# Quad 4's scores in whole tiles, quad 3's denominators ahead of them, and one load of values on another queue

## The chip, the cores and the metric

The kernel runs on one core of a Trainium2 chip. The metric is the device time of one execution in microseconds, the median of several runs. Every time below is in microseconds from the start of the profiled span unless it says otherwise.

## What is computed

Attention with a forget gate over 8 batches, 8 heads, 576 positions and 64 columns a head, then a two-layer network with a GELU on the result, seen as 4608 rows of 512:

```python
scores = (q @ k.T) / sqrt(64) + cum[:, None] - cum[None, :]    # cum = cumsum(log(clip(f, 1e-4, 1)))
attn = softmax(where(causal, -1e9, scores))
x = (attn @ v).transpose(0, 2, 1, 3).reshape(4608, 512)
h = x @ w_in                                                   # 512 x 2048
out = gelu_tanh(h) @ w_out                                     # 2048 x 512
```

## The kernel before

**Tiling.** The attention goes in 16 quads of four heads of one batch; quad i belongs to batch i // 2 and holds heads 0 to 3 (i even) or 4 to 7 (i odd). The two layers go in nine chunks of 512 rows. Chunks and quads are interleaved: the second layer of a chunk (the word F or f) is cut into small units that are put between the steps of the quads.

**The steps of a quad i**, with their words in the tables and their engines:

- LK.i, LQ.i load keys and queries through the queue of POOL (GpSimd); TK.i, TQ.i transpose them on DVE (VectorE), L197. LV.b.h loads half the heads' values of batch b through the queue of SP, LX.b.h does the same load through POOL's queue; both are five transfers, L168.
- S.i.r makes round r of the scores (r = 0, 1, 2, of 512 columns each) on PE (TensorE), L261. The four heads of a quad lie in four groups of 32 rows, and a matmul of a head uses only its own 32 rows of the array (32*128 in the profile). The result stands in two tiles of two heads each; ACT (ScalarE) takes each tile's exponential into the buffer pt (L269). H.i.r.g does the same for one pair of heads g alone. Q.i.r.g does the whole round, with pair g in a tile of another pool.
- M.i.r masks what lies beyond the diagonal on POOL (L275), m.i.r does it on DVE (L301).
- vw.i or VW.i (DVE or POOL, L214) scales the values by the gates; CL.i or cl.i copies a part of the result (L219).
- D.i sums the denominators on PE (L326), then transposes, inverts and transposes back on DVE (L345 to L349).
- V.i.x and v.i.x make the value products on PE (L326), and DVE multiplies them with the inverted denominators into xT (L357).

**The layers.** I.c.p is a product of the first layer of chunk c, 8 matmuls of 512 columns (L371) and a GELU of 1024 columns on ACT (L378). The second layer of chunk 0 has 64 units (L646): a unit of F is one matmul over the whole array, a unit of f is four matmuls of 32 columns each. Every 16 units give a block of output, which DVE copies (L652) and SP stores (L653).

**Tiles of PSUM.** Three pools hold the eight banks. psS has two tiles of two banks each, which the scores, the first layer (L371) and the product v.i.x take in turn. psO has one tile of two banks, which D.i and V.i.x share. psM has two tiles of one bank, for the second layer. A tile is taken again when its reader is done.

**Order.** The order of all work is written out by hand: FRONT (L73) for the time until chunk 1's first layer, and TABLES for the rest. Each engine and each DMA queue carries out its instructions in the order of the words. A word with @ waits until the transfer, or the step, named behind it is done: LX.1.1@WO.2 starts when the piece WO.2 of w_out has landed, VW.3@m.3.1 after the mask m.3.1.

What the change touches: the order in FRONT, the words H, S, Q (scores, L242), I (mlp_in, L360, where `spare` puts the tile into psO), LX and LV (load_v, L164).

Of the kernel before, what the change touches and what calls it, by code (L numbers as in the profile page):

```python
# [16 lines left out]
def kernel(  # L17
# [12 lines left out]
    B, H, S, D = q.shape  # L30
# [44 lines left out]
        H.1.0.1 H.1.0.0 vw.1.0 D.0.0 M.1.0.1 M.1.0.0 LP.3 WI.4 WI.5 B.2.384 H.1.1.1 V.0.0.0 H.0.1.1 V.0.1.0 H.0.1.0 D.1.0 V.1.0.0 M.0.1 WI.6 WI.7  # L75
        H.1.1.0 V.1.1.0 M.1.1 Q.0.3.0 h.0.0.0 h.0.0.0 M.0.3 LQ.2 LK.2 Q.1.3.1 h.0.0.1 h.0.0.1 vw.0.1 S.1.2 M.1.3@vw.0.1 VW.1.1 WO.0 D.0.1 j.0.1 j.0.1
        j.0.1 j.0.1 E.0.0 j.0.1 V.0.1.1 V.0.0.1 D.1.1 J.0.2 WO.1 V.1.1.1 V.1.0.1 J.0.3 w.1 J.1.0 WO.2@WI.7 WO.3 J.1.1 TQ.2 LK.3 LQ.3 J.1.2 J.1.3
        LX.1.0@WO.0 LQ.4 TK.2 X F.0.7 LK.4 TK.3 S.2.0 M.2.0 LK.5 F.0.9 S.2.2 M.2.2 LX.1.1@WO.2 F.0.10 S.2.1 TQ.3 F.0.9 LV.2.0@LK.5 m.2.1 vw.2 S.3.0
        f.0.1 CL.2 LQ.5 M.3.0 D.2 TK.4 f.0.6 S.3.1 F.0.6 m.3.1 VW.3@m.3.1 V.2.0 TQ.4 S.3.2 TK.5 LK.6 M.3.2 f.0.7 V.2.1 S.4.1 LQ.6 F.0.6 TQ.5 CL.3
        H.4.2.1 D.3 H.4.0.1 LQ.7 VW.4 H.4.0.0 V.3.1 v.3.0 f.0.3 H.4.2.0 CL.4 I.1.0 m.4.1 U.0 LV.2.1@LQ.5 I.1.4 TQ.6 m.4.2.3 I.1.1 I.1.5 U.1  # L80
        LV.3.0@LQ.7 LV.3.1 m.4.2.2 TK.6 G.0 M.4.0 LK.7 LQ.8 LK.8 I.1.2 I.1.3 U.3 K.1.0 K.1.1 K.1.2 I.1.6 I.1.7 G.1.1.2 U.2 X F.1.16 S.5.0 f.1.26 S.5.1
        D.4 M.5.0 f.1.16 S.5.2 V.4.0 m.5.2.3 f.1.10 VW.5 V.4.1 K.1.3 CL.5 m.5.2.2 S.6.0 f.1.10 M.5.1 D.5 f.1.7 S.6.1 V.5.1 f.1.12 V.5.0 T.2 S.6.2 vw.6
    """

    HOMES = {1: 0, 3: 1, 0: 2}
# [41 lines left out]
    def many(n, shape, dtype, name):  # L127
        return [singles.tile(shape, dtype, name=f"{name}{i}") for i in range(n)]
# [10 lines left out]
    vw = many(2, [128, NT + 1, 4, D], BF16, "vw")  # L139
# [15 lines left out]
    spare = singles.tile([1, 1], FP32, name="spare")  # L155
# [204 lines left out]
    def mlp_in(c, prs, spare=0):  # L360

        if spare:
            tiles = [psO.tile([128, 1024], FP32, name="ps_h", tag="po").rearrange("p (a n) -> p a n", a=2) for _ in prs]
        else:
            tiles = [psS.tile([128, 2, 512], FP32, name="ps_h", tag="s") for _ in prs]
        for pr, ph in zip(prs, tiles):
            for dts in (range(N_DT - 1), range(N_DT - 1, N_DT)):
                for j in range(2):
                    ft = 2 * pr + j
                    for dt in dts:  # L370
                        nc.tensor.matmul(  # L371
                            ph[:, j, :],
                            w_in_sb[:, dt, 128 * ft:128 * ft + 128],
                            xT[:, dt, CH * c:CH * (c + 1)],
                            start=(dt == 0), stop=(dt == N_DT - 1),
                        )
        for pr, ph in zip(prs, tiles):
            nc.scalar.activation(gT[:, 2 * pr:2 * pr + 2, :], ph, AF.Gelu_apprx_tanh)  # L378
# [111 lines left out]
    def mlp_in_half(half, g, spare=0):  # L490

        if spare:
            ph = psO.tile([128, 1024], FP32, name="ps_h", tag="po").rearrange("p (a n) -> p a n", a=2)
        else:
            ph = psS.tile([128, 2, 512], FP32, name="ps_h", tag="s")
        n0 = QA * half
        for j in range(4):
            ft = 4 * g + j
            for dt in range(N_DT):
                nc.tensor.matmul(  # L500
                    ph[:, j // 2, QA * (j % 2):QA * (j % 2) + QA],
                    w_in_sb[:, dt, 128 * ft:128 * ft + 128],
                    xT[:, dt, n0:n0 + QA],
                    start=(dt == 0 and j % 2 == 0), stop=(dt == N_DT - 1),
                    skip_group_check=True,
                )
            if j < 3:
                yield
        if spare:
            yield  # L510
        nc.scalar.activation(gT[:, 4 * g:4 * g + 4, n0:n0 + QA],
                             ph.rearrange("p a (b n) -> p (a b) n", n=QA), AF.Gelu_apprx_tanh)
# [212 lines left out]
    def pull(it, n):  # L725
        for _ in range(n):
            if next(it, False) is False:
                return
# [14 lines left out]
    def load_values(b, half):  # L743
# [29 lines left out]
        "LP": lambda t: load_v(0, ts=(t,), eng=nc.gpsimd),  # L773
        "WI": load_w_in,
        "WO": load_w_out,
        "I": lambda c, pr: mlp_in(c, (pr,)),
        "J": lambda half, g: pull(mlp_in_half(half, g), 4),
        "j": lambda half, g: pull(parts_in.setdefault((half, g), mlp_in_half(half, g, 1)), 1),
        "Q": lambda i, r, *other: scores(i, r, other=other),
# [90 lines left out]
```

## Time and profile before

| what | value |
|---|---|
| median of 3 runs | 318.97 (318.74 to 319.11) |
| the profiled execution | 319.03 |
| its span, first to last instruction | 317.3 |
| PE busy | 310.3 (98%) |
| DVE busy | 249.0 (78%) |
| ACT busy | 206.6 (65%) |
| POOL busy | 116.8 (37%) |

By stretch, around the change (busy time of each engine, share of the DMA engines): from 40.0 to 48.0, PE 7.84, DVE 4.47, ACT 5.66, POOL 6.09, DMA 1.08; from 48.0 to 56.6, PE 8.40, DVE 8.46, ACT 5.82, POOL 5.42, DMA 0.92; from 56.6 to 63.2, PE 6.48, DVE 5.44, ACT 4.92, POOL 5.79, DMA 0.90.

How to read it: the busy times of the engines overlap. The chain of waits goes back from the last instruction to what released it, step by step, and so gives the work that set the end. The busy time of an engine off that chain costs nothing by itself. A row of the timeline or of the chain has its start, its length, the engine, the line, and what is written from what; "x16" counts matmuls, and a few per cent of matmul records are missing.

### The profile page before, as it was taken

How to read it: one execution, taken by the hardware profiler on the slowest of the kernel's cores; microseconds unless marked ns; L12 is line 12 of the kernel's file. 1: busy time of each engine (PE TensorE's matmuls, PEld its weight loads, DVE VectorE, ACT ScalarE, POOL GpSimd, SP SyncE). 2: the span in 40 equal slices, each digit the busy share in tenths (PEclk: the TensorE clock that was granted, in tenths of full speed). 3: DMA queues.
4: the chain of work that ended last, by engine and by line, in shares of the span. 5: the costliest groups of instructions: out<-in, count | busy, mean ns of one | idle time of the engine just before them, and what ended most of it. 6: DMA issues, size and time to landing. Idle time of an engine off the chain costs nothing.

```text
span 317.3 us, 12367 instructions
## 1 busy us (share of the span) xinstructions
PE 310.3 (98%) x5533; PEld 218.6 (69%) x5553; DVE 249.0 (78%) x398; ACT 206.6 (65%) x266; POOL 116.8 (37%) x165
## 2 busy tenths in 40 slices
PE   8999999999999999999999999999999999999995
PEld 4468744545776477766867777768767788788784
DVE  6776059877789899779987998689878878886872
ACT  4795777676766786759756865778567844723730
POOL 8996475820500219601770068104850240000000
PEclk9999999999999999999999999999999999999999
DMA  7999999898104820791149512971120102013013
GB/s 127 230 200 199 206 225 230 171 193 175 43 22 127 138 65 19 151 222 33 37 97 197 111 37 68 170 168 37 37 68 0 37 25 80 3 34 101 0 35 99
DMA packets 47573, 33.45 MB, mean 105 GB/s; under 512 B 29856, under 2 KB 42272, under 8 KB 47520
## 3 DMA queue, kind: packets, MB, share of 16 engines
q0 software_dynamic: 9712, 15.99, 29.0%
q1 hardware_dynamic: 37664, 16.60, 19.8%
q8 instruction: 43, 0.70, 0.9%
q14 instruction: 10, 0.08, 0.1%
q10 hardware_dynamic: 144, 0.07, 0.1%
HBM read 36.85 MB, written 9.44 MB: 146 GB/s over the span
## 4 chain that ended last, share of the span: by engine, by line
PE 93%; DMA 2%; DVE 1%; issue 1%; POOL 1%; ACT 0%; POOLq 0%; DVEq 0%
PE ps_w L574 31%; PE ps_h L371 16%; PE po L326 10%; PE ps_s L261 9%; PE ps_cd L431 8%; PE ps_ab L431 6%; PE pso L646 4%; PE ps_h L500 4%; DMA q_c<-in_q_dram 2%; PE ps_h L385 2%; PE po_m L312 1%; PE ps_q L523 1%; PE ps_o L326 0%; DVE qT L197 0%; POOL k_c L191 0%
## 5 line engine op out<-in xcount | busy, mean ns | idle before, releaser
L269 ACT ACTIVATE pt<-ps_s 128x1024 bf16<-128x1024 f32 (+2 forms) x98 | 92.4, 992 | 36.2 <-PE ps_s L261 31.8
L275 POOL TENSOR_SCALAR_AFFINE_SELECT pt<-pt 128x512 bf16<-128x512 bf16 (+2 forms) x69 | 40.5, 597 | 100.3 <-ACT pt L269 99.2
L371 PE MATMUL ps_h<-xT,w_in_sb 128*128 128x512 bf16 x228 | 54.5, 379 | 0.6
L574 PEld LDWEIGHTS <-gT 128*32 128x32 bf16 (+1 forms) x1247 | 50.5, 97 | 6.0 <-issue 1.7
L574 PE MATMUL ps_w<-w_out_sb,gT 128*32 128x256 bf16 (+1 forms) x1050 | 46.9, 273 | 0.0
L378 ACT ACTIVATE gT<-ps_h 128x1024 bf16<-128x1024 f32 x30 | 30.6, 1019 | 19.5 <-PE ps_h L371 19.3
L371 PEld LDWEIGHTS <-w_in_sb 128*128 128x128 bf16 x240 | 23.4, 98 | 24.3 <-issue 0.4
L574 PEld LDWEIGHTS <-gsum 128*32 128x32 bf16 (+1 forms) x1256 | 39.1, 97 | 1.5
L261 PE MATMUL ps_s<-qT,kT 32*128 32x448 bf16 (+5 forms) x880 | 35.0, 261 | 0.6 <-DVE qT L197 0.4
L214 POOL TENSOR_TENSOR vw<-v_nat,wT 128x1280 bf16<-128x1280 f32 (+1 forms) x13 | 29.8, 2290 | 4.1 <-DVE xT L357 3.0
L574 PE MATMUL ps_w<-usum,gsum 128*32 128x256 bf16 (+1 forms) x832 | 30.5, 273 | 0.0
L197 DVE STREAM_TRANSPOSE kT<-k_c 128x576 f32<-128x576 f32 x16 | 19.9, 1241 | 11.8 <-DMA k_c<-in_k_dram 11.8
L599 DVE TENSOR_TENSOR o_st<-ps_w,snap 128x512 f32<-128x512 f32 x31 | 21.2, 686 | 9.7 <-PE ps_w L574 8.1
L261 PEld LDWEIGHTS <-kT 32*128 32x128 bf16 x896 | 15.9, 92 | 17.2 <-issue 12.0
L431 PEld LDWEIGHTS <-w_in_sb 128*128 128x128 bf16 x240 | 23.5, 98 | 5.7
L440 ACT ACTIVATE gT<-snap 128x512 bf16<-128x512 f32 x45 | 26.2, 627 | 0.6
L357 DVE TENSOR_TENSOR xT<-po,rb 128x576 bf16<-128x576 f32 x26 | 19.5, 750 | 3.8 <-PE po L326 3.2
L326 PE MATMUL po<-pt,vw 128*32 128x64 bf16 (+4 forms) x624 | 22.4, 278 | 0.0
L326 PEld LDWEIGHTS <-vw 128*32 128x32 bf16 x672 | 14.0, 96 | 10.5 <-issue 4.1
L431 PEld LDWEIGHTS <-xT 128*128 128x128 bf16 x180 | 17.6, 98 | 4.4
L197 DVE STREAM_TRANSPOSE qT<-q_c 128x576 f32<-128x576 f32 x16 | 19.9, 1243 | 0.7 <-DMA q_c<-in_q_dram 0.7
L191 POOL DMA_DIRECT2D k_c<-in_k_dram x16 | 9.2, 577 | 25.0 <-DVE qT L197 21.0
(115 smaller groups left out, 485.9 us busy)
## 6 DMA issues: line engine op xcount, KB each, us to landing
out_dram<-o_st SPq DMA_DIRECT2D x35, 256.0 KB, 2.5
k_c<-in_k_dram POOLq DMA_DIRECT2D x16, 288.0 KB, 6.1
q_c<-in_q_dram POOLq DMA_DIRECT2D x16, 288.0 KB, 6.8
v_nat<-in_v_dram SPq DMA_DIRECT2D x16, 256.0 KB, 6.5
v_nat<-in_v_dram SPq DMA_DIRECT2D x20, 128.0 KB, 5.7
w_in_sb<-in_moe_w_in_dram POOLq DMA_DIRECT2D x8, 256.0 KB, 6.3
w_out_sb<-in_moe_w_out_dram POOLq DMA_DIRECT2D x4, 512.0 KB, 9.7
v_nat<-in_v_dram POOLq DMA_DIRECT2D x9, 128.0 KB, 7.3
```

Source lines behind the costliest of these rows:

```text
L197: nc.vector.transpose(out=dst.rearrange("p s c -> p (s c)").bitcast(FP32) .rearrange("p (t a) -> p a t", a=S // 32), in_=src.rearrange("p ...
L214: return eng.tensor_mul(vw[i % 2][:, t0:t1], vb[:, t0:t1, h0:h0 + 4, :], wT[:, i, t0:t1, :].unsqueeze(3).to_broadcast([128, t1 - t0, 4, D]))
L261: nc.tensor.matmul(tiles[h // 2][:, h % 2, c0:c0 + nq], key_columns(i, key, h, c), qq[32 * h:32 * h + 32, q0:q0 + nq, c], start=(c == 0 an ...
L269: nc.scalar.activation(p[:, 2 * g:2 * g + 2, off:off + n], t[:, :, 0:n], AF.Exp, scale=scale)
L275: return nc.gpsimd.affine_select(out=x, in_=x, compare_op=ALU.is_ge, fill=0.0, base=0, pattern=pattern, channel_multiplier=-1)
L326: nc.tensor.matmul(po[r0:r0 + w.shape[-1], 448 + q0:448 + q0 + nq], w, p[:, h, col:col + nq], start=(key in (0, "low")), stop=(key in ("lo ...
L371: nc.tensor.matmul(ph[:, j, :], w_in_sb[:, dt, 128 * ft:128 * ft + 128], xT[:, dt, CH * c:CH * (c + 1)], start=(dt == 0), stop=(dt == N_DT ...
L378: nc.scalar.activation(gT[:, 2 * pr:2 * pr + 2, :], ph, AF.Gelu_apprx_tanh)
L431: nc.tensor.matmul(ps[:, j], w[:, dt, 128 * j:128 * j + 128], x[:, dt], start=(first and j == 0 and dt == 0), stop=(dt == 1), skip_group_c ...
L440: nc.scalar.activation(gT[:, ft:ft + 2, HC * j:HC * (j + 1)], x, AF.Gelu_apprx_tanh)
L574: nc.tensor.matmul(ps[c0:c0 + width, n, cols[0]:cols[1]], x[:, j, 128 * n + c0:128 * n + c0 + width], w[:, j, cols[0]:cols[1]], start=(fir ...
L599: nc.vector.tensor_add(st, ps, kept[name])
```

## The change

In FRONT:

1. Around quad 4, the four half scores H.4.2.1, H.4.0.1, H.4.0.0 and H.4.2.0 become two whole ones, S.4.2 and Q.4.0.1. Q.4.0.1 has heads 2 and 3 in the tile of psO. D.3 comes ahead of S.4.2. The nine units of the second layer there (F.0.6 and f.0.3) are cut into F.0.3, F.0.2, f.0.2 and f.0.2.
2. TQ.5 and LQ.7 move behind the product v.3.0. M.3.2 moves ahead of LK.6.
3. I.1.1 becomes I.1.1.1: its tile is taken from psO instead of psS. For that, the word I gets the argument `spare`.
4. The units of the second layer ahead of S.2.2 and of S.2.1 change places: F.0.10 and F.0.9 instead of F.0.9 and F.0.10.
5. LX.1.1@WO.2, the load of the second half of batch 1's values, becomes LV.1.1@WO.3: through SP's queue instead of POOL's, and after another piece of w_out.

The number of units of the second layer is 64 before and after.

```diff
-LX.1.0@WO.0 LQ.4 TK.2 X F.0.7 LK.4 TK.3 S.2.0 M.2.0 LK.5 F.0.9 S.2.2 M.2.2 LX.1.1@WO.2 F.0.10 S.2.1 TQ.3 F.0.9 LV.2.0@LK.5 m.2.1 vw.2 S.3.0
-f.0.1 CL.2 LQ.5 M.3.0 D.2 TK.4 f.0.6 S.3.1 F.0.6 m.3.1 VW.3@m.3.1 V.2.0 TQ.4 S.3.2 TK.5 LK.6 M.3.2 f.0.7 V.2.1 S.4.1 LQ.6 F.0.6 TQ.5 CL.3
-H.4.2.1 D.3 H.4.0.1 LQ.7 VW.4 H.4.0.0 V.3.1 v.3.0 f.0.3 H.4.2.0 CL.4 I.1.0 m.4.1 U.0 LV.2.1@LQ.5 I.1.4 TQ.6 m.4.2.3 I.1.1 I.1.5 U.1
+LX.1.0@WO.0 LQ.4 TK.2 X F.0.7 LK.4 TK.3 S.2.0 M.2.0 LK.5 F.0.10 S.2.2 M.2.2 LV.1.1@WO.3 F.0.9 S.2.1 TQ.3 F.0.9 LV.2.0@LK.5 m.2.1 vw.2 S.3.0
+f.0.1 CL.2 LQ.5 M.3.0 D.2 TK.4 f.0.6 S.3.1 F.0.6 m.3.1 VW.3@m.3.1 V.2.0 TQ.4 S.3.2 TK.5 M.3.2 LK.6 f.0.7 V.2.1 S.4.1 LQ.6 F.0.3 CL.3 D.3 F.0.2
+S.4.2 VW.4 V.3.1 f.0.2 v.3.0 TQ.5 LQ.7 f.0.2 Q.4.0.1 CL.4 I.1.0 m.4.1 U.0 LV.2.1@LQ.5 I.1.4 TQ.6 m.4.2.3 I.1.1.1 I.1.5 U.1 LV.3.0@LQ.7 LV.3.1
...
-        "I": lambda c, pr: mlp_in(c, (pr,)),
+        "I": lambda c, pr, spare=0: mlp_in(c, (pr,), spare),
```

More of the change, by code (lines that the diff above doesn't have):

```diff
@@ L77 @@
         j.0.1 j.0.1 E.0.0 j.0.1 V.0.1.1 V.0.0.1 D.1.1 J.0.2 WO.1 V.1.1.1 V.1.0.1 J.0.3 w.1 J.1.0 WO.2@WI.7 WO.3 J.1.1 TQ.2 LK.3 LQ.3 J.1.2 J.1.3
-        LX.1.0@WO.0 LQ.4 TK.2 X F.0.7 LK.4 TK.3 S.2.0 M.2.0 LK.5 F.0.9 S.2.2 M.2.2 LX.1.1@WO.2 F.0.10 S.2.1 TQ.3 F.0.9 LV.2.0@LK.5 m.2.1 vw.2 S.3.0
-        f.0.1 CL.2 LQ.5 M.3.0 D.2 TK.4 f.0.6 S.3.1 F.0.6 m.3.1 VW.3@m.3.1 V.2.0 TQ.4 S.3.2 TK.5 LK.6 M.3.2 f.0.7 V.2.1 S.4.1 LQ.6 F.0.6 TQ.5 CL.3
-        H.4.2.1 D.3 H.4.0.1 LQ.7 VW.4 H.4.0.0 V.3.1 v.3.0 f.0.3 H.4.2.0 CL.4 I.1.0 m.4.1 U.0 LV.2.1@LQ.5 I.1.4 TQ.6 m.4.2.3 I.1.1 I.1.5 U.1
-        LV.3.0@LQ.7 LV.3.1 m.4.2.2 TK.6 G.0 M.4.0 LK.7 LQ.8 LK.8 I.1.2 I.1.3 U.3 K.1.0 K.1.1 K.1.2 I.1.6 I.1.7 G.1.1.2 U.2 X F.1.16 S.5.0 f.1.26 S.5.1
-        D.4 M.5.0 f.1.16 S.5.2 V.4.0 m.5.2.3 f.1.10 VW.5 V.4.1 K.1.3 CL.5 m.5.2.2 S.6.0 f.1.10 M.5.1 D.5 f.1.7 S.6.1 V.5.1 f.1.12 V.5.0 T.2 S.6.2 vw.6
+        LX.1.0@WO.0 LQ.4 TK.2 X F.0.7 LK.4 TK.3 S.2.0 M.2.0 LK.5 F.0.10 S.2.2 M.2.2 LV.1.1@WO.3 F.0.9 S.2.1 TQ.3 F.0.9 LV.2.0@LK.5 m.2.1 vw.2 S.3.0
+        f.0.1 CL.2 LQ.5 M.3.0 D.2 TK.4 f.0.6 S.3.1 F.0.6 m.3.1 VW.3@m.3.1 V.2.0 TQ.4 S.3.2 TK.5 M.3.2 LK.6 f.0.7 V.2.1 S.4.1 LQ.6 F.0.3 CL.3 D.3 F.0.2
+        S.4.2 VW.4 V.3.1 f.0.2 v.3.0 TQ.5 LQ.7 f.0.2 Q.4.0.1 CL.4 I.1.0 m.4.1 U.0 LV.2.1@LQ.5 I.1.4 TQ.6 m.4.2.3 I.1.1.1 I.1.5 U.1 LV.3.0@LQ.7 LV.3.1
+        m.4.2.2 TK.6 G.0 M.4.0 LK.7 LQ.8 LK.8 I.1.2 I.1.3 U.3 K.1.0 K.1.1 K.1.2 I.1.6 I.1.7 G.1.1.2 U.2 X F.1.16 S.5.0 f.1.26 S.5.1 D.4 M.5.0 f.1.16
+        S.5.2 V.4.0 m.5.2.3 f.1.10 VW.5 V.4.1 K.1.3 CL.5 m.5.2.2 S.6.0 f.1.10 M.5.1 D.5 f.1.7 S.6.1 V.5.1 f.1.12 V.5.0 T.2 S.6.2 vw.6
     """
```

## The prediction, made before the changed kernel was run

> **What bounds the kernel now.** I read the page first, then the chain that ended last, then each engine's timeline from 40 to 80 us, and the DMA view in short windows. The chain:
>
> ```profile
> PE 93%; DMA 2%; DVE 1%; issue 1%; POOL 1%; ACT 0%; POOLq 0%; DVEq 0%
> ```
>
> TensorE sets the end; the clock row is full throughout. So an edit counts by what it does to PE's sequence, or by a new wait in it. Around the change the chain is PE without a break:
>
> ```profile
> 55.99 0.57 PE ps_s L261 x16
> 56.56 0.16 issue
> 56.72 1.24 PE pso L646 x5
> 57.96 0.56 PE ps_s L261 x7
> 58.52 0.80 PE po L326 x24
> 59.32 1.08 PE ps_s L261 x18
> 60.40 0.80 PE po L326 x24
> 61.19 0.73 PE ps_o L326 x24
> 61.92 0.65 PE pso L646 x12
> 62.57 0.56 PE ps_s L261 x8
> 63.13 0.32 PE ps_h L371
> ```
>
> In words of the table these are S.4.1, F.0.6 (two rows), H.4.2.1, D.3, H.4.0.1 with H.4.0.0, V.3.1, v.3.0, f.0.3, H.4.2.0 and the start of I.1.0. (Some matmul records are missing, so counts fall short of 24 or 6.) A half score of two heads (0.56) costs as much as a whole one of four (0.57): the heads sit in different rows of the array and run side by side, so half a score leaves half the rows empty. At 17.4 us a whole score with its tiles in two pools (ps_s and ps_so) runs its heads interleaved likewise.
>
> **The reworked stretch.** Prices: F.0.10 took 2.26 us (42.47 to 44.73) and F.0.6 1.40 (56.56 to 57.96), so a unit of the second layer is 0.86/4 = 0.215 and entering it from narrow work costs 0.11. f units are 0.65/3 = 0.217. Products take 0.80 after a score or an F, 0.68 after an f (55.31 in the chain). A whole score takes 0.57, its round 0 with 24 matmuls 0.63 (47.42 and 78.85).
>
> - Before, end of S.4.1 to I.1.0: 63.13 - 56.56 = 6.57.
> - After: F.0.3 0.75, D.3 0.80, F.0.2 0.54, S.4.2 0.57, V.3.1 0.80, f.0.2 0.43, v.3.0 0.68, f.0.2 0.43, Q.4.0.1 0.63 = 5.63.
>
> That is 0.94 less: four half scores (2.20) become two whole ones (1.20), two products lose a little, and one more entry into F costs 0.11. The nine units of F and f are the same work.
>
> Now the waits. S.4.2 needs both score buffers, so both exponentials of S.4.1, which end at 58.53 (ACT runs them 0.97 each from 56.59); PE gets there at 56.56 + 2.09 = 58.65. Cover 0.1. V.3.1 needs the product tile that D.3's transpose on DVE reads: D.3 ends at 58.1, the transpose takes 0.78, PE arrives at 59.2. Cover 0.3; DVE is free then, since TQ.5 (1.23) now stands behind it and DVE idled 0.95 there before. v.3.0 needs S.4.2's first exponential: 60.25 against PE's 60.45. Q.4.0.1 needs the second one (61.2) and the product tile (V.3.1's multiplication, 60.9), PE arrives at 61.56. Each is covered, none by more than 0.7. Each cover that fails costs its shortfall.
>
> Then the first layer. ACT's four exponentials end at 64.0 or so, as before (64.19), then a table load of 1.28; so the first GELU starts near 65.3, hardly earlier than 65.51. PE is about 1 us earlier, so it needs room: I.1.1 in the product tile gives it a third buffer. Three products of 1.73 from 62.0 end at 67.2, the first GELU at 66.3. Cover 0.9.
>
> **The two words before it.** At S.2.2 PE waits:
>
> ```profile
> 41.59 0.25 PE ps_s L261 x2
> 41.83 0.00 issue
> 41.84 0.63 PE ps_s L261 x8
> ```
>
> From 41.59 to 42.47 is 0.88 where a whole score takes 0.57: 0.31 goes on ACT's exponential, which ends at 41.78. F.0.10 ahead of it in place of F.0.9 puts 0.215 of work into that wait, and the unit is missing after it: 0.21 gained, if S.2.1 finds its buffers free (its exponentials end at 44.46, PE would come at 44.5). Between nothing and 0.21 I take 0.21.
>
> **The load that changes queue.** LX.1.1, five loads of v on POOL (3.63 us at 45.77), goes to SP as LV.1.1, once WO.3 has landed (about 40.0). POOL issues LQ.5 earlier; nothing waited for POOL there, so the 3.63 are worth nothing by themselves. What counts is when the load lands, because of this sequence on POOL:
>
> ```profile
> 54.21 2.33 POOL L214 TENSOR_TENSOR vw<-v_nat,wT 128x1280 bf16<-128x1280 f32 x1 [2.98 <-DVE xT L357]
> 56.50 0.59 POOL L191 DMA_DIRECT2D k_c<-in_k_dram  x1
> 57.09 1.24 POOL L275 TENSOR_SCALAR_AFFINE_SELECT pt<-pt 128x512 bf16<-128x512 bf16 x2
> ```
>
> VW.3, LK.6, M.3.2. The wait ahead of VW.3 is put down to DVE, but its other gate m.3.1 ended at 53.4, and the last piece of LX.1.1, issued at 48.8, landed 5.3 later, at 54.1: the load is what it waits for. D.3 now wants M.3.2's result a microsecond earlier. The swap of M.3.2 with LK.6 returns 0.59: VW.3 from 54.2 gives M.3.2 done at 57.8, and D.3's last pieces come up at about 57.75. So the point is a landing at 54.1: earlier is free, later stops PE for the excess. Four queue rows bear on it (packets, MB, share), first 52 to 54 us, then 54 to 56:
>
> ```profile
> q0 software_dynamic: 110, 0.23, 68.4%
> q1 hardware_dynamic: 271, 0.07, 18.0%
> ```
>
> ```profile
> q1 hardware_dynamic: 1472, 0.36, 83.1%
> q0 software_dynamic: 43, 0.07, 20.5%
> ```
>
> SP's loads of v go in 256-byte packets (512 a load, 2304 for LV.1.1) and crawl while POOL's queue (q0) is busy, 135 a us, then run at 736. From 40 to 49.4 q0 is full (97.8%). From 69 to 72 both moved well together: 171 and 1394 packets. Bounds: 465 a us as there, with 2 us until the first packet: 47; 135 a us throughout: 57. If no engine time is lost, all that is queued (9.4 us of q0, 1.4 for LQ.5, 3.2 for LV.1.1) is done by 54.0, and LV.1.1 isn't the last of it. I take 52, halfway between the bounds, since both kinds of row occur; VW.3 then starts at m.3.1's end, 53.3.
>
> [...]
>
> Further on: LQ.7 now waits for TQ.5 (to about 63.1), with M.4.0 and LK.7 behind it on POOL; M.4.0 is needed by D.4 at 83, and LV.3.0, gated by LQ.7, stands on SP behind LV.2.1, which keeps SP until 69 anyway. TQ.5 pushes DVE's U.0 to TK.6 later by some 0.4 where DVE has 2.01 idle before G.0. The output store is off the path.
>
> **Sum.** 0.94 + 0.21 = 1.15. The profiled execution took 319.03 (span 317.3 and 1.7 around it), 0.06 above the median; the median becomes 318.97 - 1.15 = **317.8**.
>
> **Rivals.**
> 1. *POOL becomes the bound (slower).* LV.1.1 lands at 57 instead of 52; M.3.2, behind VW.3, ends at 57 + 2.33 + 1.24 = 60.6 and D.3 at 60.8 instead of 57.9: 2.9 lost, 1.15 gained, 320.7. It decides from a landing at 55.3 (no gain); 55.9 is measurably slower. For it: the 135 a us. Against: the busy stretch of q0 ends near 52.
> 2. *SP's load pushes POOL's loads.* LX.1.0 (last piece issued at 37.6, landed 7.8 later, at 45.4) comes up to 3.2 us later, 48.6, and vw.2, which would start at 47.5, is 1.1 late. DVE has no idle time from 47.34 to 58.42, so V.2.1's multiplication ends at 57.85 and D.3, in the same tile, starts 0.75 late: 318.6. For it: q0 is full. Against: it takes the whole 3.2 on exactly these loads.
> 3. *The gain comes back at the first layer.* If I.1.1 doesn't get its tile early, PE waits for the first GELU, about 0.85: 318.7. Against: the 0.9 of cover above.
> 4. *The whole score isn't whole*: Q's halves in two pools run one after the other, +0.6: 318.4. Against: 17.4 us.
>
> **Chances.** Forecast 0.58 (317.4 to 318.3); rivals 2 and 4 together 0.20, a third of that still beyond 0.2%; rival 3 and other lost covers 0.09; rival 1 0.13. 0.2% (0.64 us, about what a measurement of this kernel can tell from no change) puts the bounds at 318.33 and 319.61: faster 0.65, same 0.22, slower 0.13. The range 317.4 to 318.9 leaves out rival 1, the upper end of the small losses, and some 0.02 below.
>
> **What would show it.** Right: two score groups of 16 and 24 matmuls between S.4.1 and I.1.0, that stretch at 5.6 us, D.3 directly behind F.0.3, S.2.2 without its 0.31, VW.3 at 53.3. Wrong: idle PE ahead of D.3 with M.3.2 late (rival 1) or with V.2.1's multiplication late (2), a gap at I.1.1 or I.1.5 (3), score groups of over 1 us (4).

## The result, and the profile after

| | before | after |
|---|---|---|
| median, 8 runs each | 319.10 | 318.28 (318.07 to 318.56) |
| ratio after to before | | 0.9971, 95% interval 0.9961 to 0.9980 |
| profiled execution | 319.03 | 318.36 |
| its span | 317.3 | 316.6 |

The kernel became 0.82 us faster (0.29%), where 1.15 was forecast: 318.28 against 317.8, inside the range of 317.4 to 318.9. The chain that ended last, by engine:

```profile
PE 84%; DMA 10%; POOL 2%; issue 1%; SPq 1%; ACT 0%; DVE 0%; POOLq 0%; DVEq 0%
```

PE had 93% before. The rest is one new link: the chain now leaves PE in the middle of D.3 and goes back through POOL to SP's load. The chain up to 61.7 us, from the load on (start, length, what; ... stands for rows left out):

```profile
43.58 10.54 DMA v_nat<-in_v_dram
...
54.28 1.27 POOL vw L214
...
57.16 0.64 POOL pt L275
57.80 0.04 issue
57.84 0.28 PE po L326 x8
58.13 0.54 PE pso L646 x2
58.66 0.56 PE ps_s L261 x16
59.23 0.80 PE po L326 x24
60.02 0.43 PE pso L646 x8
60.45 0.81 PE ps_o L326 x24
61.27 0.43 PE pso L646 x8
```

Read it from the top: the last piece of LV.1.1 (issued at 43.58, landed at 54.12), VW.3, M.3.2's second mask until 57.80, and only then D.3's last eight matmuls. Below that the order is the new one, with the whole score S.4.2 at 0.56. The two groups of POOL behind the load, from POOL's timeline:

```profile
54.28 2.33 POOL L214 TENSOR_TENSOR vw<-v_nat,wT 128x1280 bf16<-128x1280 f32 x1 [3.26 <-DMA v_nat<-in_v_dram]
56.57 1.22 POOL L275 TENSOR_SCALAR_AFFINE_SELECT pt<-pt 128x512 bf16<-128x512 bf16 x2
```

The wait of 3.26 is now put down to the load itself. PE's timeline shows what it costs, and S.2.2 without the wait of before:

```profile
41.67 0.73 PE L261 MATMUL ps_s<-qT,kT 32*128 32x320 bf16 x16
...
57.02 1.11 PE L326 MATMUL po<-pt,w_bf 128*32 128x512 bf16 x24
58.06 0.60 PE L646 MATMUL pso<-w_out_sb,gT 128*128 128x512 bf16 x2
```

D.3 takes 1.04 from its start to the next group where it took 0.80 (58.45 to 59.25) before. S.2.2 takes 0.73 instead of 0.95. The queue rows from 42 to 50 us, while SP's load and POOL's loads run side by side:

```profile
q0 software_dynamic: 588, 1.27, 78.3%
q1 hardware_dynamic: 2074, 0.51, 35.9%
```

SP moved 259 packets a us there, between the forecast's 135 and 465.

To compare kernels below the noise of whole runs, I cut PE's timeline at starts that all kernels have: S.2.0, S.4.1, the first layer (I.1.0), and the second layer of chunk 1 (L574). D.3 is given as its start to the start of the next group.

| kernel | S.2.0 to S.4.1 | S.4.1 to I.1.0 | of it D.3 | the rest of it | I stretch |
|---|---|---|---|---|---|
| before | 17.08 | 7.14 | 0.80 | 6.34 | 13.88 |
| after | 16.92 | 6.56 | 1.04 | 5.52 | 13.82 |
| after_again | 16.92 | 6.31 | 0.80 | 5.51 | 13.83 |
| swap_alone | 16.92 | 7.13 | 0.79 | 6.34 | 13.89 |
| load_on_pool | 16.90 | 6.32 | 0.79 | 5.53 | 13.83 |
| half_score | 16.93 | 6.45 | 0.93 | 5.52 | 13.82 |
| halves_apart | 16.91 | 6.89 | 0.84 | 6.05 | 13.82 |
| whole_in_before | 17.09 | 7.56 | 0.80 | 6.76 | 13.88 |
| mask_on_dve | 16.92 | 6.44 | 0.92 | 5.52 | 13.82 |
| late_load | 16.92 | 7.72 | 2.19 | 5.53 | 13.83 |
| early_load | 16.93 | 6.39 | 0.88 | 5.51 | 13.83 |
| own_tiles | 16.92 | 7.98 | 0.80 | 7.18 | 13.81 |
| no_third_tile | 16.91 | 6.81 | 1.30 | 5.51 | 14.79 |
| pool_and_more | 16.92 | 6.59 | 1.11 | 5.48 | 13.81 |

Behind the I stretch all of them need 236.9 or 237.0 us more on PE, so nothing is given back later. Ahead of S.2.0 they differ by up to 0.6 (38.59 to 39.22) without a pattern by edit.

### The profile page after: what moved, and what is told of

Same layout as the page of the kernel before. It is cut to its first block, busy times and chain, and to the rows that moved or that the text cites. A ratio compares the mean times of both kernels' runs of the same rounds, so it can differ in the third digit from the quotient of the medians.

```text
span 316.6 us, 12394 instructions
## 1 busy us (share of the span) xinstructions
PE 311.3 (98%) x5556; PEld 218.3 (69%) x5556; DVE 250.0 (79%) x398; ACT 206.4 (65%) x266; POOL 114.4 (36%) x160
## 4 chain that ended last, share of the span: by engine, by line
PE 84%; DMA 10%; POOL 2%; issue 1%; SPq 1%; ACT 0%; DVE 0%; POOLq 0%; DVEq 0%
PE ps_w L574 31%; PE ps_h L371 16%; PE po L326 9%; PE ps_cd L431 8%; PE ps_s L261 7%; PE ps_ab L431 6%; DMA w_out_sb<-in_moe_w_out_dram 4%; DMA v_nat<-in_v_dram 3%; DMA w_in_sb<-in_moe_w_in_dram 3%; PE idle_ps L239 2%; PE ps_h L385 2%; SPq L168 1%; POOL pt L275 1%; POOL w_in_sb L180 1%; ACT pt L269 0%
## 5 line engine op out<-in xcount | busy, mean ns | idle before, releaser
L269 ACT ACTIVATE pt<-ps_s 128x1024 bf16<-128x1024 f32 (+2 forms) x97 | 91.4, 992 | 35.9 <-PE ps_s L261 33.9
L275 POOL TENSOR_SCALAR_AFFINE_SELECT pt<-pt 128x512 bf16<-128x512 bf16 (+2 forms) x69 | 41.5, 611 | 101.7 <-ACT pt L269 100.3
L371 PE MATMUL ps_h<-xT,w_in_sb 128*128 128x512 bf16 x240 | 55.1, 379 | 0.0
L574 PEld LDWEIGHTS <-gT 128*32 128x32 bf16 (+1 forms) x1247 | 50.5, 97 | 6.0 <-issue 1.7
L574 PE MATMUL ps_w<-w_out_sb,gT 128*32 128x256 bf16 (+1 forms) x1050 | 46.9, 273 | 0.0
L574 PEld LDWEIGHTS <-gsum 128*32 128x32 bf16 (+1 forms) x1256 | 39.1, 97 | 1.4
L261 PE MATMUL ps_s<-qT,kT 32*128 32x64 bf16 (+5 forms) x868 | 33.8, 262 | 0.1
L574 PE MATMUL ps_w<-usum,gsum 128*32 128x256 bf16 (+1 forms) x832 | 30.5, 273 | 0.0
```

The source lines that it names most:

```text
L261: nc.tensor.matmul(tiles[h // 2][:, h % 2, c0:c0 + nq], key_columns(i, key, h, c), qq[32 * h:32 * h + 32, q0:q0 + nq, c], start=(c == 0 an ...
L269: nc.scalar.activation(p[:, 2 * g:2 * g + 2, off:off + n], t[:, :, 0:n], AF.Exp, scale=scale)
L275: return nc.gpsimd.affine_select(out=x, in_=x, compare_op=ALU.is_ge, fill=0.0, base=0, pattern=pattern, channel_multiplier=-1)
L371: nc.tensor.matmul(ph[:, j, :], w_in_sb[:, dt, 128 * ft:128 * ft + 128], xT[:, dt, CH * c:CH * (c + 1)], start=(dt == 0), stop=(dt == N_DT ...
L574: nc.tensor.matmul(ps[c0:c0 + width, n, cols[0]:cols[1]], x[:, j, 128 * n + c0:128 * n + c0 + width], w[:, j, cols[0]:cols[1]], start=(fir ...
```

## Experiments: the score tiles

**half_score** undoes the whole tile of S.4.2 in place.

```diff
-S.4.2 VW.4 V.3.1
+H.4.2.0 H.4.2.1 VW.4 V.3.1
```

> The changed kernel with S.4.2 made again as two half scores, in the same place and the same tiles. Theory (half a score costs PE as much as a whole one, since the other row groups idle): two groups of 8 matmuls, 0.56 each, the stretch from S.4.1 to the first layer 0.56 longer, the time 0.5 above the changed kernel, 318.8. Rival (the gain came from moving D.3 and cutting the second layer's units, the halves cost nothing by themselves): no change, 318.3.

Measured: ratio to the kernel before 0.9976 (0.9963 to 0.9988), as the changed kernel within the intervals. The two halves, in PE's timeline:

```profile
58.81 0.65 PE L261 MATMUL ps_s<-qT,kT 32*128 32x320 bf16 x16
59.39 0.87 PE L326 MATMUL po<-pt,vw 128*32 128x512 bf16 x24
```

Sixteen matmuls in 0.58 from start to start: two halves next to each other cost one whole score. The prediction's reading, that each half fills PE for the time of a whole one, fell here. But then H.4.0.1 and H.4.0.0, neighbours in the kernel before, should have taken some 0.6 and not 1.08. ACT's row of before, three exponentials, says why:

```profile
56.59 3.06 ACT L269 ACTIVATE pt<-ps_s 128x1024 bf16<-128x1024 f32 x3 [0.87 <-PE ps_s L261]
```

It ends at 59.65, and the second of those halves uses the tile that the third exponential frees. So I formed another theory, W: a half costs a whole score's time only where it stands alone, and 0.45 of the 1.08 (all but the 0.63 of a whole round 0) was a wait for ACT.

**whole_in_before** puts W against the prediction's reading, within the kernel before.

```diff
-H.4.2.1 D.3 H.4.0.1 LQ.7 VW.4 H.4.0.0 V.3.1
+H.4.2.1 D.3 LQ.7 VW.4 S.4.0 V.3.1
```

> The kernel before with nothing but its two neighbouring half scores H.4.0.1 and H.4.0.0 made as one whole score S.4.0, in the same two tiles. Theory W (their 1.08 us in the chain is 0.63 of matmuls and 0.45 of waiting for ACT's exponential of H.4.2.1, which holds the second tile until 59.65): the whole score starts 0.45 later and ends at the same time, V.3.1 still at 60.33, the time equals the kernel before. Theory R, the one of the prediction (each half occupies PE for the time of a whole score): the group takes 0.63, everything behind it 0.45 earlier, 318.5.

Measured: ratio 1.0013 (1.0003 to 1.0022), slower. PE's timeline:

```profile
59.41 0.20 PE L261 MATMUL ps_s<-qT,kT 32*128 32x64 bf16 x2
59.86 0.69 PE L261 MATMUL ps_s<-qT,kT 32*128 32x64 bf16 x22 [0.25 <-ACT pt L269]
60.48 0.87 PE L326 MATMUL po<-pt,vw 128*32 128x512 bf16 x24
61.65 0.87 PE L326 MATMUL ps_o<-pt,vw 128*32 128x512 bf16 x24 [0.31 <-ACT pt L269]
```

Two matmuls, then a wait for ACT, then the other 22: 1.07 from 59.41 to 60.48, the 1.08 of the two halves. W holds in the score itself; that the time would equal the kernel before did not. What I had not expected is the last line: a whole score finishes its first tile later, so its first exponential comes later, and v.3.0, which takes that tile, waits: 1.17 from V.3.1 to v.3.0 instead of 0.73. In the old order a whole score was worth less than nothing.

**halves_apart** tests the other half of W.

```diff
-D.3 F.0.2
-S.4.2 VW.4
+D.3 F.0.1
+H.4.2.0 F.0.1 H.4.2.1 VW.4
```

> The changed kernel with S.4.2 made as two half scores that one unit of the second layer keeps apart (F.0.1, half, F.0.1, half in place of F.0.2 and the whole). Theory W (a half costs a whole score's time only where it stands alone): one more group of 0.56 and one more entry into F of 0.11, less the 0.12 that v.3.0 waited for the first exponential: the stretch from S.4.1 to the first layer 0.55 longer, time 318.8. Rival (row groups of the array overlap across the unit of F as well): no change, 318.3.

Measured: ratio 1.0007 (0.9990 to 1.0024). The rest of the stretch takes 6.05 instead of 5.52, 0.53 more, W's figure. PE's timeline:

```profile
58.58 0.63 PE L261 MATMUL ps_s<-qT,kT 32*128 32x320 bf16 x8
59.14 0.39 PE L646 MATMUL pso<-w_out_sb,gT 128*128 128x512 bf16 x1
59.46 0.63 PE L261 MATMUL ps_s<-qT,kT 32*128 32x320 bf16 x8
60.02 0.87 PE L326 MATMUL po<-pt,vw 128*32 128x512 bf16 x24
```

Each half, eight matmuls, takes 0.56 from start to start, as long as the sixteen together above.

**own_tiles** takes the value products' banks away from the score.

```diff
-Q.4.0.1 CL.4
+S.4.0 CL.4
```

> The changed kernel with S.4.0 in place of Q.4.0.1: both tiles from the scores' own pool, none from the value products' banks. Theory (the banks matter, because the score's second tile is otherwise v.3.0's, free only after DVE's multiplication at 62.1, and the first layer's first product would need the tile of S.4.0's first exponential): 0.45 of wait in the score and some 0.9 ahead of the first layer's first product, 319.6. Rival (only whole tiles matter, the pool doesn't): 318.3.

Measured: ratio 1.0030 (1.0020 to 1.0039), 320.19 against 318.56 for the changed kernel on the same chip. PE's timeline:

```profile
61.34 0.20 PE L261 MATMUL ps_s<-qT,kT 32*128 32x64 bf16 x2
61.84 0.69 PE L261 MATMUL ps_s<-qT,kT 32*128 32x64 bf16 x22 [0.30 <-DVE xT L357]
63.63 2.53 PE L371 MATMUL ps_h<-xT,w_in_sb 128*128 128x512 bf16 x11 [1.10 <-ACT pt L269]
```

The score waits for v.3.0's multiplication, the first layer for the score's exponential: 7.18 instead of 5.51 for the rest of the stretch, 1.67, where some 1.35 was expected. The tile of psO is what makes the new order possible; the whole score without it loses twice what the change gains.

**no_third_tile** gives I.1.1 a tile of psS again.

```diff
-I.1.1.1 I.1.5
+I.1.1 I.1.5
```

> The changed kernel with I.1.1 in the scores' pool again. Theory, the third rival's price in the prediction: PE waits for the first GELU (ends 66.6) ahead of the third product of the first layer, which it reaches at 65.7: 0.85 lost, 319.15. Rival (PE is held up by the second layer's end or the gelu pace anyway): no change.

Measured: ratio 1.0003 (0.9992 to 1.0013), 319.28 against 318.56. The I stretch takes 14.79 instead of 13.83, 0.96 where 0.85 was priced. PE's waits from 56 to 77 us (engine and line, for whom, us, times, longest):

```profile
PE ps_h L371 <- ACT gT L378: 0.8, 1, 0.8
PE po L326 <- POOL pt L275: 0.3, 1, 0.3
```

The first line is the wait for the first GELU; the second is D.3's wait for M.3.2, half a microsecond in this execution by the table.

## Experiments: the earlier words and the load

**swap_alone** is the kernel before with the two groups of the second layer exchanged.

```diff
-LK.5 F.0.9 S.2.2 M.2.2 LX.1.1@WO.2 F.0.10 S.2.1
+LK.5 F.0.10 S.2.2 M.2.2 LX.1.1@WO.2 F.0.9 S.2.1
```

> The kernel before with nothing but F.0.10 ahead of S.2.2 and F.0.9 ahead of S.2.1. Theory (a unit of second layer fills a wait for ACT): S.2.2 without its second wait, everything behind it 0.21 earlier, time 0.2 below the kernel before. Rival (the wait moves to S.2.1, whose tiles come free only at 44.46): nothing gained, equal to the kernel before.

Measured: ratio 0.9990 (0.9977 to 1.0002), not told from no change by the timing. In the profile S.2.0 to S.4.1 takes 16.92 instead of 17.08: 0.16. From S.2.0 to S.2.1 it gains 0.21 (44.58 - 38.97 = 5.61 against 44.66 - 38.84 = 5.82), and S.2.1, which now meets ACT's exponential, gives some 0.05 back (0.61 to the next group instead of 0.57, in rounded starts). The theory holds, with that much of the rival.

**load_on_pool** undoes the move between the queues.

```diff
-M.2.2 LV.1.1@WO.3 F.0.9
+M.2.2 LX.1.1@WO.2 F.0.9
```

> The changed kernel with the load LX.1.1 back on POOL's queue behind WO.2. Theory (the queue moves nothing, since the load lands at 54.1 either way and POOL is not on the path): landing at 54.1 within 0.4, VW.3 at 54.2, PE's wait within D.3 0.25 as in the changed kernel, time 318.3 within 0.2. Rival (POOL's 3.6 us of issuing matter): M.3.2 later, D.3's wait grows by over 0.5, 318.8 or more.

Measured: ratio 0.9976 (0.9962 to 0.9991), as the changed kernel. VW.3 starts at 54.02, M.3.2 ends at 57.53, and D.3, from 57.45, takes 0.79: no wait in this execution, where 0.25 was expected. The queue moves nothing that the timing shows.

**after_again** is the changed kernel beside the others.

> The changed kernel itself, beside the three others on the same chip. Expected 0.8 to 0.9 us below the kernel before. Since the load's landing varies from run to run while VW.3 follows it, the wait in D.3 may differ from 0.25: it should be VW.3's end plus 1.22 of masks less D.3's own pace, between 0 and 0.3.

Measured: ratio 0.9979 (0.9967 to 0.9991). POOL's and PE's timelines:

```profile
53.96 2.33 POOL L214 TENSOR_TENSOR vw<-v_nat,wT 128x1280 bf16<-128x1280 f32 x1 [3.03 <-DVE xT L357]
```

```profile
56.94 0.87 PE L326 MATMUL po<-pt,w_bf 128*32 128x512 bf16 x24
57.74 0.61 PE L646 MATMUL pso<-w_out_sb,gT 128*128 128x512 bf16 x2
```

The same program, VW.3 at 53.96 instead of 54.28, and D.3's wait is gone. So the wait of 0.24 in the first profile belongs to that execution: over the kernels of the new order and with the load on either queue, VW.3 starts between 53.71 and 54.74 (late_load apart), and D.3 takes between 0.79 and 1.30.

**late_load** prices that wait.

```diff
-LV.1.1@WO.3
+LV.1.1@LQ.4
```

> The changed kernel with LV.1.1 held back until LQ.4 has landed (about 48.5 instead of 40.6). First rival of the prediction, as a price: the load lands some 2 to 4 us later, VW.3 starts with it, M.3.2 ends 3.6 later than the landing, and D.3 with it; the time grows by the landing's excess over 53.9, that is to 320 to 322, and VW.3, not V.2.1's multiplication, is what D.3 waits for. Rival (SP's packets only crawl while POOL's queue is busy, so a later start costs nothing): landing at 54.1 again, 318.3.

Measured, in one execution: 319.34. SP starts the load at 47.06 instead of 40.61, and VW.3 starts at 55.25 instead of 54.28. POOL, then PE:

```profile
55.25 2.33 POOL L214 TENSOR_TENSOR vw<-v_nat,wT 128x1280 bf16<-128x1280 f32 x1 [4.41 <-DMA v_nat<-in_v_dram]
57.54 1.22 POOL L275 TENSOR_SCALAR_AFFINE_SELECT pt<-pt 128x512 bf16<-128x512 bf16 x2
```

```profile
56.84 0.62 PE L326 MATMUL po<-pt,w_bf 128*32 128x512 bf16 x12
58.22 0.31 PE L326 MATMUL po<-pt,w_bf 128*1 128x320 bf16 x4 [0.77 <-POOL pt L275]
58.81 0.28 PE L326 MATMUL po<-pt,w_bf 128*1 128x192 bf16 x8 [0.28 <-POOL pt L275]
```

The first rival's mechanism is all there: M.3.2 ends at 58.76, D.3's last blocks start at 58.81, D.3 takes 2.19. Against S.4.1's start VW.3 is 1.16 later than in the changed kernel, D.3 1.15 longer: one for one. The size of the delay was missed: 6.45 us of later start moved the landing by only 1, from 54.12 to 55.09.

The ten profiles of the new order with both masks on POOL lie on one line: where VW.3 starts 1.66 or more ahead of S.4.1, D.3 takes 0.79 or 0.80 (load_on_pool 2.10, own_tiles 1.94, after_again 1.66), and otherwise it takes longer by what is missing from 1.66, within 0.01 (the changed kernel 1.42 and 1.04, no_third_tile 1.16 and 1.30, late_load 0.26 and 2.19).

**early_load** starts it sooner.

```diff
-LV.1.1@WO.3
+LV.1.1@WO.2
```

> The changed kernel with LV.1.1 behind WO.2 instead of WO.3, so that it starts near 38.4 instead of 40.6. If the landing follows the start, VW.3 begins at m.3.1's end, 53.3, and D.3 loses its wait of 0.25: 318.05. Rival (the load is paced by what POOL's queue leaves over, not by its start): landing within 0.5 of 54.1, D.3's wait as before, 318.3; and if SP's packets push POOL's loads, TQ.3 or vw.2 late and 318.5 or more.

Measured: ratio 0.9992 (0.9980 to 1.0005), not told from no change. SP's row for the load, first in the changed kernel, then here:

```profile
40.61 5.61 SPq L168 DMA_DIRECT2D v_nat<-in_v_dram  x5
```

```profile
38.21 10.80 SPq L168 DMA_DIRECT2D v_nat<-in_v_dram  x5
```

The load starts 2.4 us earlier and lands at 54.13 instead of 54.12; VW.3 starts at 54.30, D.3 takes 0.88. The rival holds: here the start doesn't set the landing.

**mask_on_dve** takes half of M.3.2 off POOL.

```diff
-TK.5 M.3.2 LK.6 f.0.7 V.2.1 S.4.1
+TK.5 M.3.2.2 LK.6 f.0.7 V.2.1 m.3.2.3 S.4.1
```

> The changed kernel with the second half of M.3.2 (key block 3) as a product on DVE ahead of S.4.1, so that POOL's part ends 0.6 earlier. Theory (PE waits 0.25 in D.3 for POOL's last mask, behind VW.3, behind the load): the wait goes, D.3 back to 0.80, the first layer 0.25 earlier, time 318.05. Rival (D.3 is limited by its own matmuls or by DVE's transpose of the tile): D.3 unchanged, 318.3; if DVE's extra 0.42 delays the transpose of D.3, up to 318.5.

Measured: ratio 0.9988 (0.9964 to 1.0012), inconclusive by timing. In the profile the one mask left on POOL takes 0.92 (56.52), where two took 1.22, so it ends at 57.44 and D.3 takes 0.92. Of the gain of 0.25, about half arrived. Why the mask slowed down isn't shown; DVE's mask (56.54) and copy (56.97) run at the same time.

**pool_and_more** aims at both waits that are left.

```diff
-M.2.2 LV.1.1@WO.3 F.0.9
+M.2.2 LX.1.1@WO.2 F.0.9
...
-V.3.1 f.0.2 v.3.0 TQ.5 LQ.7 f.0.2 Q.4.0.1
+V.3.1 f.0.3 v.3.0 TQ.5 LQ.7 f.0.1 Q.4.0.1
```

> The changed kernel with LX.1.1 back on POOL's queue behind WO.2 and with f.0.3 ahead of v.3.0 and f.0.1 behind it, instead of two and two. If the two remaining waits are what the stretch is short of the forecast (0.25 in D.3 for M.3.2, 0.12 ahead of v.3.0 for the first exponential): both go, from S.4.1 to the first layer 6.20 instead of 6.56, time 0.3 below the changed kernel. Rival (v.3.0 a unit later makes its multiplication late, and the first layer's first product waits for that tile): 6.3, 0.2 below the changed kernel at most.

Measured: ratio 0.9992 (0.9971 to 1.0013), not told from no change; from S.4.1 to the first layer it is 6.59, where 6.20 was hoped for. D.3 takes 1.11, since VW.3 starts at 54.48 with the load on POOL's queue too. The rest of the stretch takes 5.48 instead of 5.51: v.3.0 no longer waits (0.65 for the three units ahead of it), but the first layer starts 0.72 after the score instead of 0.63. The rival holds, and no version here beats the changed kernel clear of the noise.

## Why the prediction came out as it did

- **PE sets the end; the stretch around quad 4 is what counts: right.** The profile's gain is 0.16 ahead of S.4.1, 0.58 from there to the first layer, 0.06 in the I stretch.
- **The sum of the stretch, 5.63 instead of 6.57: the size was off.** Without D.3's wait it gained 0.82 to 0.83 (7.14 to 6.31 in after_again) instead of 0.94. The missing 0.12 is the cover at v.3.0, given there as 0.2. S.4.2's first exponential starts at 59.33 and takes 1.02, not 0.97, so it ends at 60.35; V.3.1 and f.0.2 take 0.69 (priced at 0.80) and 0.43 from start to start and reach v.3.0 at 60.28; it starts at 60.40. In pool_and_more, with a third unit ahead of v.3.0, this wait is gone.
- **Half a score costs as much as a whole one: right for halves that stand alone, wrong for neighbours.** half_score, halves_apart and whole_in_before show it. The price survived since it was taken from the chain, where the 1.08 of the neighbours contained ACT's wait of 0.45; the cause given for that part was wrong. Of the 1.00 that the scores gained (2.20 to 1.20), 0.45 is that wait and 0.55 the two halves that stood alone. The new order removes the wait by leaving ACT time (D.3 and F.0.2 ahead of S.4.2) and by the tile of psO (own_tiles: 1.67 without it). No run moves D.3 alone, so its own share isn't shown.
- **S.2.2's wait, 0.21: nearly right.** 0.16 arrived; S.2.1 gave back 0.05, at the condition that the prediction named.
- **The load lands at 52 and D.3 is free: wrong.** It landed at 54.12, and D.3 lost 0.24 in that profile; over the profiles of the new order (late_load apart) it is between nothing and 0.5. So the first rival came true in its mechanism, with a tenth of its price. The point where it begins was given as a landing at 54.1. In this profile it is 53.9: VW.3 would have to start at 54.04, 1.66 ahead of S.4.1, and starts 0.16 after the landing. The point was worked out from S.4.1 as it was before, and the 0.2 gained ahead of it brings D.3 forward by as much. The room of 2 us that the prediction gave the load was not there at all; that the loss stayed small is luck, since the landing came to lie so near the point. late_load shows the slope.
- **The second rival: in small, and off PE's path.** POOL's next loads, LQ.4 and LK.4, took 7.4 and 7.6 from issue to landing; they took 6.2 each before, and in late_load, where SP's load began only behind LQ.4. LX.1.0, which the rival named, hardly paid: its last piece landed 8.0 after its issue instead of 7.8, and vw.2 started at 47.45. TQ.3 waited 0.98 for its load and started at 44.27 instead of 42.81, but SP's load isn't the cause: in late_load TQ.3 waited 1.06, to 44.04, and SP's load began at 47.06. The prediction's early bound for the landing, 47 (465 packets a us), was far off: the load landed at 54.12, and from 42 to 50 us SP's queue moved 2074 packets and 0.51 MB, POOL's 588 packets and 1.27 MB.
- **The third rival: no.** The I stretch took 13.82. no_third_tile puts its price at 0.96, where 0.85 was forecast.
- **The fourth: no.** Q.4.0.1 takes 0.63, one interleaved group.

So 0.82 + 0.16 + 0.06 = 1.04 where every load is early, and 0.8 with the wait of the first profile; the measured 0.82 lies there. From the forecast's side, 1.15 less 0.05 (S.2.1), 0.12 (v.3.0) and 0.24 (D.3), plus the 0.06 of the I stretch, is 0.80. The 0.06 wasn't forecast, and its cause isn't shown. How often the load is late enough in unprofiled runs wasn't measured.

## What to carry to other kernels

A long row in the chain can be work and waits together (the 1.08 of the two halves held 0.45 of waiting): before a price is explained, look for the wait inside it, above all where an instruction's second tile is still being read. A larger unit finished its first part later here, and what waited for that part paid (v.3.0 in whole_in_before: 1.17 instead of 0.73); whole tiles gained here only with a spare bank (in own_tiles, without it, the stretch took 1.67 longer) and other work ahead of them. Covers of 0.1 to 0.3 us are no covers when one of the two sides is a transfer whose landing varies as it did here: VW.3, which follows the load, started between 1.16 and 2.10 us ahead of S.4.1 over the profiles of the new order (late_load apart).

## What the runs showed of the hardware

Two neighbouring half scores of eight matmuls each, in different 32-row parts of the array, took 0.58 together (half_score), one that stood alone 0.56 (halves_apart): next to each other they overlapped. A load of 576 KB in 256-byte packets on SP's queue, beside POOL's queue (78.3% of the engines' time from 42 to 50 us in the changed kernel), landed at 54.1 us whether it began at 38.2 (early_load) or 40.6 (the changed kernel), and at 55.1 when it began at 47.1 (late_load). By 50 us SP's queue had moved 0.51 MB in the changed kernel (the load has 2304 packets of 256 bytes, 0.59 MB), and yet its last piece landed at 54.12. From 50 to 52 us SP's queue moved 213 packets with 0.23 MB, a mean of 1.1 KB, so mostly the output stores that SP had issued behind the load. What holds the last packets back stays open.
